# A linear-attention and gated-FFN kernel on one core: batch 0's first k blocks loaded and worked in smaller pieces, loads in another order, the last output in two column parts, and a new work order

## The chip, the cores and the metric

The kernel runs on one core of a Trainium2 chip. The metric is device time in microseconds, the median of several executions. Beside the times there is one profiled execution, with its trace.

## What is computed

For each of 8 batches and 8 heads there are 576 tokens of 64 numbers in q, k and v. A feature map turns q and k into 256 features, linear attention is done with these, and the result (4608 tokens of 512 numbers) goes through a gated FFN.

```
def phi(x):
    proj = einsum('bhsd,df->bhsf', x, w_phi)          # 64 -> 128
    proj = proj - max(abs(proj), axis=-1)
    return concatenate([exp(proj), exp(-proj)])       # 256 features
q_p, k_p = phi(q), phi(k)
kv  = einsum('bhsf,bhsd->bhfd', k_p, v);  z = sum(k_p, axis=2)
num = einsum('bhsf,bhfd->bhsd', q_p, kv); den = einsum('bhsf,bhf->bhs', q_p, z) + 1e-06
x   = (num / den), heads side by side                 # (4608, 512)
out = (maximum(x @ w_gate, 0) * (x @ w_val)) @ w_out  # d_ff = 1536
```

## The kernel before

Matmuls are in bfloat16. All work is cut into small steps called atoms. Each is registered with a number, and a long string, `ORDER`, names the numbers in the order in which the instructions are emitted. As every engine works through its own queue in order, this string fixes the order on TensorE, VectorE, ScalarE, GpSimd and in the DMA queues (SyncE's and GpSimd's) alike. An apostrophe behind a number picks the other engine for a step that two can do, and `z4` emits four fill matmuls of zeros (line 197).

**k of batches 0 and 1.** The 576 tokens of a pair of heads lie as nine blocks (`CP`) of 128 rows, so a batch has four pairs (`NU`) and 36 blocks (`NB`). `k_batch` cuts them into items of eight blocks, 8, 8, 8, 8 and 4. The atoms of item u of batch b are:

- `kT` transposes on TensorE (line 268); `kTc` copies the result to SBUF as tile tT (line 281), on VectorE, or on ScalarE with the apostrophe.
- `kr` projects with w (line 309), into two PSUM banks; `km` takes the row maxima mk on VectorE (line 316), one for each bank; `ke` takes exp of plus and minus the projection on ScalarE (line 365), into tile kp.
- `kk` takes exp of plus and minus the maxima on ScalarE (line 376), tile ek; `vs` scales v by ek (lines 325 and 407), on GpSimd, or on VectorE with the apostrophe.
- `kv` (line 501) multiplies kp with vs, two pairs at a time, over all their blocks; `kvc` (line 415) copies the result.

The tiles kp and vs come from rings of five buffers each. In batches 2 to 7 the transposes are done by DMA and an item is two heads (line 478 for `kv`).

**q.** A `q_item` covers half of a batch's 512 main tokens per head. `qT`, `qTc` are transposes and copies (batches 0 and 1 only); `qc` (line 539) and `qr` (line 309) project, once for the exponentials `qe` (line 557) and once for the maxima `qm` (line 316); `qk` (line 573) is the correction; `n` (line 587) multiplies with kv; `nt` (line 606) and `nu` (line 618) combine the two halves on VectorE; `xu` (lines 625 and 627) divides; `xT` and `xc` (line 647) turn the result for the FFN on TensorE, or `xd` (line 635) by DMA. The last 64 tokens of every head go through tail items and a ninth FFN group.

**FFN.** For each group g, `fv` and `fg` (matmuls at line 717) multiply by w_val and w_gate; `fv` copies on ScalarE or VectorE (line 732), `fg` multiplies on VectorE (line 739); `fo` (line 765) multiplies by w_out in three thirds, and the last third copies the result (line 775) and stores it. In group 0 the first four chunks are done on half of the tokens each (`FIRST`). The weights come through GpSimd's DMA queue in thirds: `wv0`, `wg0` and so on. The last store (group 8, t = 3) is issued in two halves of 64 rows, on SyncE's and ScalarE's queues (line 750).

**The first loads.** Batch 0's k and v come in fp32 over SyncE's queue, k of a pair ahead of its v. GpSimd's own loads (all with a cast) are held back by a tiny copy:

```
for lo, hi in ((0, 1), (1, 2), (2, NU)):
    load_pairs(0, "kn", k, nc.sync, FP32, lo, hi, buf="vn1")
    load_pairs(0, "vn", v, nc.sync, FP32, lo, hi, buf="vn0")
...
gate = singles.tile([P, 1], FP32)
nc.gpsimd.tensor_copy(gate, inputs["kn", 0][:, CP * D : CP * D + 1])
for par in range(2):
    nc.vector.tensor_copy(w2[half_rows(par)], wf)
```

The element that `gate` reads is the first of pair 1. In the trace the fp32 k tile goes by the name of its buffer, vn, as v does.

Of the kernel before, what the change touches and what calls it, by code (L numbers as in the profile page):

```python
# [8 lines left out]
FP32 = mybir.dt.float32  # L9
# [7 lines left out]

FIRST = ((0, 2, 0, 4), (2, 4, 0, 4), (0, 4, 4, 12))

LAST = ((0, 512),)  # L20
# [3 lines left out]
ORDER = """z4 82 83' z1 84 87 86 92 7 8 0 93' 88 85 89 z1 94 95 97 122 123 102 112 1 96 124 98 103 104 99 113  # L24
108 127 90 125 129 105 114 118 91 107 109 115 106 z5 138 100' 177 101 117 139 141 128 126 116 140
178 143 119 186 188 130 142 111 190 110 132 133' 144 145 146 148 147 151 134 150 149 10 120 180 184
152 179 121 131 182 135 137' 153 181 165 154 166 155 167 136 156 29 185 2 159 157 3 191 183 160 187
54 158 226 161 227' 9 171 172 162 168 169 173 216 217' 170 198 199 174 236 256 257 228 192 200 193
189 195 196 237' 194 197 163 164' 246 247' 311 207 208 175 176 209 210 211 201 272 204 205 312' 232
212 206 213 1082' 1083 1084 273' 1085 1086 231 4 1087 1088 202 203 214 215' 218 314 229 233 316 318  # L30
222 1089 1090' 1091 1092 1093 5 220 221 1094 1095 230 219 1096 1097 1098 238 242 239 6 258 259 248
260 261 263 11 223 241 252 243 1099 1100' 250 234 251 240 1101 1102' 249 225 1103 262 1104 1105 320
322 224 324 253 280 244' 254' 284 274 276 282 1106' 1107 1108 1109 264 278 1110 313 255 275 279 317
245 235 266 277 267' 268 281 285 283 30 315 265 269 270 13 351 355 350 319 325 271 321 323 1111
1112' 353 1113 341 338 339 344 342 343 39 1114 1115 340 329 330 345 352 326 331 332 333 354 346 334
299 1116 327 347 305 286 290 291 1117 287 12 328 363 306 356 1118 300 335 51 302 364 365 307 288
1119 303 304 301 308 348 349 293 40 289 1120 1121 292 360 1122 294 295 296 309 310' 361 362 336
1123 388 398 400 337 14 368 371 31 297 298 1124 369 399 372 390 1125 1126 401 16 41 403 389 370 404
1127 1128 402 373 1129 374' 33 58 62 378 381 379 1130 1131 42 1132 405 15 391 380 383 61 393 395
1133 1134 1135 392 394 59 357 358 359 1136 1137 1138 63 415 419 414 418 416 1139 417 1140' 1141 382  # L40
60 64 1142 1143 408 412 409 411 413 410 450 452 454 1144 384 396 397 385 386 387' 375 376 444 377'
448 449 451 443 446 406 420 432 407' 1145 453 438 445 65 1146 447 433 439 440 435 427 428 436 437
455 434 441 442 1147 32 1148 473 474 470 471 472 424 425 426 1149 429 421 422 423 467 468 1150 1151
469 475 1152 456 476 459 498 477 500 460 488 501 430 462 463 464 431 457 490 1153 1154 461 458 465'
502 492 466 499 489 1155 1156 1157 525 519 521 52 503 504 523 19 527 524 528 1158 1159 529 526 1160
491 508 511 478 554 556 510 558 479 482 493 481 509 17 505 530 1161 506 507 1162' 1163 512 513 480
1164 1165 55 559 563 494 560 518 522 483 562 564 565 1166 1167 561 520 1168' 1169 484' 66 69 67 44
43 553 555 557 1170' 1171 515 514 516 517 485 495 496 486 487' 1172' 497 583 577 1173 68 36 70 534
535 536 1174 22 580 581 578 366 367 584 531 579 582 532 1175 1176 566 567 568 548 549 1177 585 586
21 545 587 542 18 546 533 537 538 539 543 544 550 34 547 1178 1179 1180 1181 1182' 589 626 628 588  # L50
591 1183 551 552 569 592 590 540 541 627 1184' 629 570 631 630 1185 1186 1187 572 595 571 593 594
573 1188 574 575 71 1189 1190 576 20 596 597 636 637 616 617 620 72 606 607 619 640 609 1191 1192
1193 608 639 621 598 599 1194' 1195 1196 600 622 618 610 647 46 651 611 612 681 683 641 643 642 685
653 657 53 649 1197' 655 638 1198' 1199 1200' 1201 644 645 652 656 688 690 613 682 686 614 623 624
684 601 602 625' 615 603 692 654 1202' 1203 646 648 687 1204' 633 632 634 635' 650 691 1205 1206'
1207 1208 665 658 662 676 677 689 673 666 45 674 35 667 663 664 1209 670 671 672 1210 659 678 1211
1212 23 660 675 679 680 47 726 728 729 756 758 56 727 731 1213 1214 1215 1216 661 732' 668 669 705
693 706 707 711 712 708 1217 1218 709 710 713 730 760 1219 714 1220' 1221 746 747 736 739 733 750
715 694 695 696 740 738 748 749 700 701 702 25 1222 1223 1224' 697 698 699 703 737 741 1225 1226
704 716 719 718 720 763 73 792 794 717 796 751 767 1227 743 765 1228 1229 1230 1231 762 766 752 757  # L60
791 721 742' 764 744 795 38 759 761 768 793 1232 1233' 753 1234 1235 723 1236' 745 754 755' 734 798
735 797 26 799 722' 827 829 802 1237 1238 831 800 810 48 803 811 807 808 809 775 812 776 801 1239
# [54 lines left out]
def kernel(  # L117
# [20 lines left out]
    nc = tc.nc  # L138
# [4 lines left out]
    P = 128  # L143
# [681 lines left out]
```

## Time and profile before

| | |
|---|---|
| median of 3 runs | 381.93 us (381.91 to 382.31) |
| profiled execution | 382.19 us, of which the span of the profile 380.3 us |
| TensorE busy | 365.8 us (96%) |
| VectorE busy | 294.0 us (77%) |
| ScalarE busy | 215.2 us (57%) |
| GpSimd busy | 139.2 us (37%) |
| TensorE's granted clock, mean | 0.998 |
| DMA | 45.10 MB, mean 119 GB/s |

All times in the profile are in us from the start of the span, unless marked ns. A row of a timeline has start, length, engine, line, operation, output and inputs, count, and in brackets the idle time of the engine before it with what ended it. The length of a merged row reaches to the end of its last instruction; instructions of one engine overlap a little, so the step from one start to the next is often shorter than one instruction's length.

### The profile page before, as it was taken

The numbers are of one execution on the slowest core, as the hardware profiler recorded it, in microseconds if no ns is written. First come the engines' busy times: TensorE is split into PE (matmuls) and PEld (weight loads), VectorE is DVE, ScalarE is ACT, GpSimd is POOL, SyncE is SP. The second block draws the span as 40 slices with busy tenths as digits, with TensorE's granted clock in tenths as the row PEclk, the third lists the DMA queues.
The fourth block names the chain that finished last, engine by engine and source line by source line (L and its number), as shares of the span: only waits on it lengthen the run. The fifth ranks groups of instructions, "written<-read, shape, count | busy, mean of one in ns | idle before, by whom it ended". The sixth has DMA issues, their size and how long they took to land.

```text
span 380.3 us, 8896 instructions
## 1 busy us (share of the span) xinstructions
PE 365.8 (96%) x3447; PEld 196.7 (52%) x3495; DVE 294.0 (77%) x640; ACT 215.2 (57%) x505; POOL 139.2 (37%) x183
## 2 busy tenths in 40 slices
PE   6879999999999999999999999999999999999995
PEld 2558455545544645554555555565554544444442
DVE  3988989888887899989969987989858925836530
ACT  4998994678589647665875459771864112000111
POOL 3976462458265325722580244853400110000000
PEclk9999999999999999999999999999999999999999
DMA  7999997995359989983759743570310220021003
GB/s 245 189 181 236 197 143 149 227 212 154 28 117 196 161 242 162 175 104 73 125 113 148 202 125 96 83 82 16 97 56 16 29 97 28 2 69 55 2 27 84
DMA packets 87625, 45.10 MB, mean 119 GB/s; under 512 B 55776, under 2 KB 81440, under 8 KB 87584
## 3 DMA queue, kind: packets, MB, share of 16 engines
q1 hardware_dynamic: 59984, 30.42, 35.7%
q0 software_dynamic: 27200, 13.57, 27.8%
q10 hardware_dynamic: 400, 0.56, 0.5%
q8 instruction: 27, 0.44, 0.5%
q14 instruction: 14, 0.11, 0.1%
HBM read 37.78 MB, written 9.44 MB: 124 GB/s over the span
## 4 chain that ended last, share of the span: by engine, by line
PE 88%; ACT 4%; DVE 3%; issue 2%; DMA 1%; SPq 0%; DVEq 0%
PE pa L717 45%; PE pa L765 24%; PE pa L587 5%; PE pa L309 5%; PE pa L478 4%; PE pa L539 2%; PE pa L268 2%; DVE h L739 2%; ACT kp L365 2%; DMA vn<-in_k_dram 1%; ACT qp L557 1%; PE pa L501 1%; ACT tT L281 1%; DVE mk L316 1%; DVE val_sb L732 0%
## 5 line engine op out<-in xcount | busy, mean ns | idle before, releaser
L739 DVE SCALAR_TENSOR_TENSOR h<-pa,val_sb 128x512 bf16<-128x512 f32 (+1 forms) x112 | 74.4, 668 | 33.2 <-PE pa L717 24.1
L717 PE MATMUL pa<-xT,wg_sb 128*128 128x512 bf16 (+1 forms) x387 | 98.1, 370 | 0.7
L717 PE MATMUL pa<-xT,wv_sb 128*128 128x512 bf16 (+1 forms) x385 | 97.9, 370 | 0.6
L765 PE MATMUL pa<-wo_sb,h 128*128 128x512 bf16 x414 | 96.7, 379 | 1.2 <-issue 0.3
L732 ACT CAST val_sb<-pa 128x512 bf16<-128x512 f32 (+1 forms) x65 | 37.8, 581 | 81.7 <-PE pa L717 81.4
L557 ACT ACTIVATE qp<-pa 128x512 bf16<-128x512 f32 x144 | 76.1, 625 | 10.3 <-PE pa L539 8.3
L365 ACT ACTIVATE kp<-pa 128x512 bf16<-128x512 f32 (+1 forms) x148 | 76.7, 617 | 9.2 <-PE pa L309 7.7
L627 POOL TENSOR_TENSOR xu<-u,r 128x512 bf16<-128x512 f32 x30 | 31.6, 1058 | 119.1 <-DVE r L625 78.6
L325 POOL TENSOR_TENSOR vs<-vn,ek 128x512 bf16<-128x512 f32 (+1 forms) x58 | 60.0, 1041 | 34.0 <-ACT ek L376 28.1
L717 PEld LDWEIGHTS <-wg_sb 128*128 128x128 bf16 x448 | 41.8, 98 | 45.1 <-issue 2.1
L717 PEld LDWEIGHTS <-wv_sb 128*128 128x128 bf16 x448 | 41.8, 98 | 44.7 <-issue 1.5
L765 PEld LDWEIGHTS <-h 128*128 128x128 bf16 x432 | 40.1, 98 | 45.0 <-issue 0.3
L316 DVE TENSOR_REDUCE mk<-pa 128x4 f32<-128x512 f32 (+1 forms) x74 | 46.9, 667 | 6.0 <-PE pa L309 5.2
L316 DVE TENSOR_REDUCE mq<-pa 128x4 f32<-128x512 f32 x72 | 46.2, 681 | 5.7 <-PE pa L309 5.6
L618 DVE TENSOR_TENSOR u<-pa,t 128x195 f32<-128x195 f32 (+3 forms) x120 | 37.9, 332 | 3.3
L606 DVE TENSOR_TENSOR t<-pa,cq 128x195 f32<-128x195 f32 (+3 forms) x120 | 37.7, 326 | 3.3 <-ACT cq L573 1.5
L775 ACT COPY out_sb<-pa 128x512 f32<-128x512 f32 x21 | 12.7, 603 | 44.5 <-PE pa L765 42.5
L587 PEld LDWEIGHTS <-qp 128*128 128x128 bf16 x640 | 27.5, 98 | 12.2 <-issue 0.6
L732 DVE CAST val_sb<-pa 128x512 bf16<-128x512 f32 (+1 forms) x47 | 31.6, 673 | 2.5 <-PE pa L717 1.6
L587 PE MATMUL pa<-kv,qp 128*128 128x65 bf16 x640 | 30.0, 193 | 0.4 <-ACT qp L557 0.3
L775 DVE COPY out_sb<-pa 128x512 f32<-128x512 f32 x15 | 10.3, 689 | 21.6 <-PE pa L765 18.1
L478 PEld LDWEIGHTS <-kp 128*128 128x128 bf16 x480 | 16.4, 98 | 3.8 <-issue 1.2
(67 smaller groups left out, 273.4 us busy)
## 6 DMA issues: line engine op xcount, KB each, us to landing
out_dram<-out_sb SPq DMA_DIRECT2D x32, 256.0 KB, 2.6
vn<-in_v_dram SPq DMA_DIRECT2D x6, 1024.0 KB, 6.0
qn<-in_q_dram POOLq DMA_DIRECT2D x8, 512.0 KB, 7.5
kn<-in_k_dram POOLq DMA_DIRECT2D x6, 512.0 KB, 7.7
wv_sb<-in_moe_w_val_dram POOLq DMA_DIRECT2D x3, 512.0 KB, 6.9
wg_sb<-in_moe_w_gate_dram POOLq DMA_DIRECT2D x3, 512.0 KB, 9.0
wo_sb<-in_moe_w_out_dram POOLq DMA_DIRECT2D x1, 1536.0 KB, 15.7
vn<-in_v_dram SPq DMA_DIRECT2D x1, 1152.0 KB, 9.2
```

What stands on the lines that cost most here:

```text
L316: nc.vector.tensor_reduce(m, some.rearrange("p (c f) -> p c f", f=F), axis=AX.X, op=ALU.max, apply_absolute_value=True,)
L325: eng.tensor_tensor(dst[:, :, s, 0:D], src, ek[:, :, s : s + 1].to_broadcast(list(src.shape)), op=ALU.mult,)
L365: nc.scalar.activation(st["kp"][:, s, 0 : n // 2, par, :], st["banks"][par][:, 0 : n // 2 * F].rearrange("p (a f) -> p a f", f=F), AF.Exp, ...
L478: nc.tensor.matmul(kv_ps[:, hh, s, :], lhsT=lhsT, rhs=rhs, start=(n == 0), stop=(n == 19))
L557: nc.scalar.activation(x["qp"][:, s, slot].rearrange("p a b -> p (a b)"), st["cols", i][par], AF.Exp, scale=sign,)
L587: nc.tensor.matmul(pn[:, E * (2 * i + s) : E * (2 * i + s + 1)], lhsT=x["qp"][:, s, slot, blk, :], rhs=kv_of(b, lo + i)[:, s, :],)
L606: nc.vector.tensor_tensor(x["t", j][rows, 0:n], ab[:, :, 1], c[:, :, None].to_broadcast([np_, n, E]), op=ALU.mult,)
L618: nc.vector.tensor_tensor(x["u"][rows, lo : lo + n], ab[:, :, 0], x["t", j][rows, 0:n], op=ALU.add)
L717: nc.tensor.matmul(ps, lhsT=w[:, dc, P * fi : P * fi + P], rhs=xTs[g][:, dc, lo:hi], start=(dc == 0), stop=(dc == NDC - 1),)
L732: copy_by(copy_of(alt, "ACT", "DVE"))(st["val", n], ps)
L739: nc.vector.scalar_tensor_tensor(st["h2"][:, fi, lo:hi], ps, 0.0, st["val", n], op0=ALU.max, op1=ALU.mult)
L765: nc.tensor.matmul(po, lhsT=st["h2"][:, fi, P * t : P * t + P], rhs=wo_sb[:, fi, c0:c1], start=(fi == 0), stop=(fi == NFC - 1),)
```

## The change

- `K_CUTS` sets where the items of batches 0 and 1 are cut. Batch 0 now has six items, of 4, 4, 8, 8, 8 and 4 blocks; batch 1 keeps 8, 8, 8, 8, 4. `kv_pairs` looks up an item and a block in a list, `place`.
- Batch 0's k and v are loaded in seven DMAs instead of six: k pair 0 blocks 0 to 3, k pair 0 blocks 4 to 8, k pair 1, v pair 0, k pairs 2 and 3, v pair 1, v pairs 2 and 3.
- `gate` stands as it was, and reads from k pair 1, which is now ahead of v.
- The second half of w2 is copied by ScalarE instead of VectorE.
- The last output is done in two column parts, 352 and 160, each with its own twelve matmuls, copy and two stores (`LAST`).
- `ORDER` is new throughout. There are 9 fill matmuls instead of 11.

```
+K_CUTS = [[4, 8, 16, 24, 32], [8, 16, 24, 32]]
-LAST = ((0, 512),)
+LAST = ((0, 352), (352, 512))
...
-    def load_pairs(b, name, src, eng, dtype, lo=0, hi=NU, buf=None):
+    def load_pairs(b, name, src, eng, dtype, buf=None, pairs=slice(0, NU), toks=slice(0, CP)):
...
-            out=t.rearrange("p (u n) -> p u n", u=NU)[:, lo:hi],
+            out=t.rearrange("p (u c d) -> p u c d", u=NU, c=CP)[:, pairs, toks],
...
-        items = [
-            k_item(
+        cuts = [0] + K_CUTS[b] + [NB]
+        place = []
+        for u, (lo, hi) in enumerate(zip(cuts, cuts[1:])):
+            st = k_item(
                 b,
                 u,
-                min(8, NB - 8 * u),
-                lambda u=u: blocks(u),
+                hi - lo,
+                lambda lo=lo, hi=hi: blocks(lo, hi),
                 None,
-                lambda u=u: v_blocks(8 * u, min(8 * u + 8, NB)),
+                lambda lo=lo, hi=hi: v_blocks(lo, hi),
             )
-            for u in range(-(-NB // 8))
-        ]
+            place += [(st, c) for c in range(hi - lo)]
...
-                it, c = items[blk // 8], blk % 8
+                it, c = place[blk]
...
-    for lo, hi in ((0, 1), (1, 2), (2, NU)):
-        load_pairs(0, "kn", k, nc.sync, FP32, lo, hi, buf="vn1")
-        load_pairs(0, "vn", v, nc.sync, FP32, lo, hi, buf="vn0")
+    for name, *part in (
+        ("k", slice(0, 1), slice(0, 4)),
+        ("k", slice(0, 1), slice(4, CP)),
+        ("k", slice(1, 2)),
+        ("v", slice(0, 1)),
+        ("k", slice(2, NU)),
+        ("v", slice(1, 2)),
+        ("v", slice(2, NU)),
+    ):
+        src, buf = (k, "vn1") if name == "k" else (v, "vn0")
+        load_pairs(0, f"{name}n", src, nc.sync, FP32, buf, *part)
...
-    for par in range(2):
-        nc.vector.tensor_copy(w2[half_rows(par)], wf)
+    for par, copy in enumerate((nc.vector.tensor_copy, nc.scalar.copy)):
+        copy(w2[half_rows(par)], wf)
```

The start of both orders, with the numbers replaced by names (`ke.0.2.1` is batch 0, item 2, second bank; `ld` is a load). On ScalarE, up to the last `qe` of batch 0 and the copies behind it:

```
before: kTc.0.0' ke.0.0.0 kTc.0.1' ke.0.0.1 kk.0.0 ke.0.1.0 ke.0.1.1 kk.0.1 ke.0.2.1 kk.0.4 ke.0.3.1
  kk.0.2 ke.0.2.0 ke.0.4.1 ke.0.4.0 ke.0.3.0 kk.0.3 qe.0.0.0.0 qe.0.0.0.1 qe.0.0.1.0 kvc.0.0.1 qe.0.0.1.1
  qk.0.0 qe.0.1.0.0 kvc.0.1.0 qk.0.1 qe.0.1.0.1 qe.0.1.1.0 kTc.1.1' kTc.1.0' qe.0.1.1.1 kTc.1.2' xc.0.0'
after:  kTc.0.0' kTc.0.1' ke.0.0.0 ke.0.0.1 kk.0.1 ke.0.1.1 ke.0.1.0 kk.0.0 ke.0.2.1 ke.0.2.0 kk.0.2
  kTc.0.3' kTc.0.4' ke.0.3.1 ke.0.4.0 kk.0.3 ke.0.4.1 ke.0.3.0 kk.0.4 qe.0.0.1.1 qe.0.0.1.0 ke.0.5.0 kk.0.5
  qe.0.0.0.0 ke.0.5.1 qe.0.0.0.1 qe.0.1.0.0 qk.0.0 kvc.0.1.0 qe.0.1.0.1 kTc.1.4' qe.0.1.1.1 qk.0.1
  qe.0.1.1.0 kTc.1.0' kTc.1.3' qTc.1.1' xc.0.0'
```

On GpSimd with its loads, up to batch 0's first `xu`:

```
before: ld.q0 ld.k1 ld.wv0 ld.wg0 vs.0.0.0 vs.0.0.1 vs.0.1.1 vs.0.4.0 vs.0.2.1 vs.0.2.0 ld.q1 vs.0.3.0
  vs.0.3.1 vs.0.4.1 ld.qm0 ld.wv1 ld.wg1 xu.0.0.0
after:  ld.q0 ld.k1 vs.0.1.0 ld.wv0 ld.qm0 vs.0.2.0 vs.0.0.1 vs.0.3.0 vs.0.3.1 ld.q1 vs.0.4.0 vs.0.4.1
  vs.0.5.0 vs.0.5.1 ld.wg0 ld.wv1 ld.wg1 xu.0.0.0
```

106 lines of the change are left out of this document (42 added, 64 removed), and 29 rows, old and new, of the table ORDER.

## The prediction, made before the changed kernel was run

> **What bounds the kernel now.** I read the busy time by stretches first, then the chain that ended last, then the timelines of the first 31 us and of the last 15 us. Columns below: the stretch, its length, busy us of TensorE, weight load, VectorE, ScalarE and GpSimd, granted clock, DMA share, GB/s.
>
> ```profile
> 0.00:8.30 8.30, 5.16 (x22) 2.47 (x22) 3.78 (x7) 2.95 (x4) 2.13 (x9) 1.00 0.72 241
> 8.30:16.00 7.70, 7.14 (x60) 4.61 (x59) 6.30 (x12) 7.32 (x22) 7.05 (x11) 1.00 1.14 195
> 16.00:30.70 14.70, 11.56 (x301) 8.83 (x299) 13.03 (x38) 14.55 (x36) 10.48 (x15) 1.00 1.31 187
> 30.70:60.00 29.30, 29.05 (x379) 18.30 (x381) 26.98 (x55) 25.62 (x65) 16.65 (x22) 1.00 1.20 194
> 60.00:375.80 315.80, 312.94 (x2692) 162.47 (x2735) 243.89 (x531) 164.16 (x383) 102.92 (x128) 1.00 0.55 104
> 375.80:380.30 4.50, 0.00 (x0) 0.00 (x0) 0.00 (x0) 0.57 (x1) 0.00 (x0) 0.87 0.29 87
> ...
> 1.65 5.46 DMA vn<-in_k_dram
> 30.73 3.21 PE pa L717 x28
> 370.41 5.36 PE pa L765 x24
> 375.79 0.58 ACT out_sb L775
> ```
>
> TensorE is the bound from 30.7 us on: it idles 0.25 us of 29.3 and 2.86 us of 315.8. The rest of its idle time lies at the ends: 3.14 us before 8.3, 0.56 us to 16, 3.14 us to 30.7, and 4.5 us behind its last matmul. In the stretch from 16 to 30.7 ScalarE is busy 14.55 of 14.70 us: there the exponentials set the pace and TensorE follows. The chain begins with a load of k, pair 1, and is TensorE from 30.73, where the first FFN matmul starts. So the change can gain in three places: the time at which that matmul starts (the work put before it is the same set of matmuls in both orders, less two fill matmuls), the 3.1 us of idle time behind it, and the tail.
>
> **The loads.** The first rows of the start, and the issues of the loads with their us from issue to landing:
>
> ```profile
> 3.92 1.09 PE L268 MATMUL pa<-ident,vn 128*128 128x128 f32 x4 [1.04 <-DMA vn<-in_k_dram]
> 4.03 0.47 DVE L794 CAST w<-wf 64x128 bf16<-64x128 f32 x2 [0.72 <-DMA wf<-in_w_phi_dram]
> 5.04 0.59 ACT L281 CAST tT<-pa 128x512 bf16<-128x512 f32 x1 [2.43 <-PE pa L268]
> 5.68 0.61 PE L309 MATMUL pa<-w,tT 64*128 64x128 bf16 x8 [0.25 <-ACT tT L281]
> 6.33 1.08 ACT L365 ACTIVATE kp<-pa 128x512 bf16<-128x512 f32 x2 [0.70 <-PE pa L309]
> 7.16 0.19 POOL L792 COPY gate<-vn 128x1 f32<-128x1 f32 x1 [5.50 <-DMA vn<-in_k_dram]
> ...
> vn<-in_k_dram SPq DMA_DIRECT2D x1, 288.0 KB, 3.0
> vn<-in_v_dram SPq DMA_DIRECT2D x1, 288.0 KB, 3.4
> vn<-in_k_dram SPq DMA_DIRECT2D x1, 288.0 KB, 5.5
> ```
>
> The third load, k pair 1, was issued at 1.65 with 576 KB ahead of it and took 5.5 us. Now it is still third, but with 288 KB ahead, as the second load had, which took 3.4 us: it lands at 5.05 (4.65 by the first row, 7.15 by the third). The gate at 7.16 and GpSimd's loads behind it then move up by 2.1 us. v pair 0 takes over the later place; its reader needs the k maxima first, at about 6.6 below.
>
> The first exponential moves too. Two transposes instead of four in front of the copy save 0.54 (half of 1.09), a half-size copy 0.22 (half of 0.59, less some fixed time), half the projections 0.26 (0.61 less 0.35), and a 128 KB load instead of 288 KB at most the 0.2 us until w arrives at 4.03. 6.33 less 1.2 is 5.1. The two halves of w on two engines lie in that wait for w and are worth nothing further; without that cover the extra ScalarE copy costs it 0.24 us, half of the row of two. SP issues seven loads now; the added issue (0.50 on the ACT queue in the tail below) stands ahead of v and of k pairs 2 and 3, whose readers come behind 6.6 us; uncovered it would cost that 0.50.
>
> **ScalarE up to the last q exponential of batch 0.** Prices are the steps from one start to the next:
>
> ```profile
> 8.30 0.58 ACT L281 CAST tT<-pa 128x512 bf16<-128x512 f32 x1 [0.89 <-PE pa L268]
> 8.78 1.09 ACT L365 ACTIVATE kp<-pa 128x512 bf16<-128x512 f32 x2
> 15.01 3.17 ACT L365 ACTIVATE kp<-pa 128x512 bf16<-128x512 f32 x8
> 17.97 0.40 ACT L376 ACTIVATE ek<-mk 128x8 f32<-128x8 f32 x2
> 18.17 3.12 ACT L557 ACTIVATE qp<-pa 128x512 bf16<-128x512 f32 x6
> 21.03 0.53 ACT L415 CAST kv<-pa 128x260 bf16<-128x260 f32 x1
> 21.28 1.26 ACT L557 ACTIVATE qp<-pa 128x512 bf16<-128x512 f32 x2
> ...
> 27.97 0.68 ACT L281 COPY tT<-pa 128x512 bf16<-128x512 bf16 x1
> 30.03 0.41 DVE L647 COPY xT<-pa 128x512 bf16<-128x512 bf16 x1
> ```
>
> Six q exponentials take 2.86 (18.17 to 21.03), so 0.48 each and 0.96 a pair. Of the eight of k from 15.01 to 17.97 four are of four blocks: (2.96 - 4 x 0.48)/4 = 0.26 each, 0.52 a pair. A pair of ek is 0.20, a kv copy 0.25, a copy of transposes 0.48. Before, ScalarE took 19.67 us from its second copy at 8.30 to the end of its last q exponential, where the copy at 27.97 follows. In the new order that stretch, begun at the first exponential, has four more half pairs and one full pair less (+2.08 - 0.96), one more ek pair (+0.20), one kv copy less (-0.25), and of copies two fp32 and a half more against three fewer (0.96 + 0.27 - 3 x 0.48 = -0.21, the half one an estimate): +0.86, so 20.53 us. From 5.1 that ends at 25.6; with 0.5 us for its new small waits (the first ek now wants VectorE's maxima of the second item, and the sixth k item wants the first one's buffer of a ring of five, which the first kv product frees) 26.1 against 27.97: 1.8 us earlier. Behind it two copies of 512 columns and one of 1024 (1.9, as four of 0.48) stand before the xT copy (0.48) that now releases the FFN; that still puts the release at 28.5, against the VectorE copy that started at 30.03, ended at 30.44 and released the matmul at 30.73.
>
> **GpSimd is the nearer bound.** The last kv product of batch 0 wants GpSimd's last v product, which ended at 21.59:
>
> ```profile
> 19.68 1.05 POOL L325 TENSOR_TENSOR vs<-vn,ek 128x512 bf16<-128x512 f32 x1
> 20.67 0.25 POOL L407 CAST vs<-ek 128x16 bf16<-128x16 f32 x1
> 20.82 0.61 POOL L325 TENSOR_TENSOR vs<-vn,ek 128x256 bf16<-128x256 f32 x1
> 21.38 0.21 POOL L407 CAST vs<-ek 128x8 bf16<-128x8 f32 x1
> L211 POOL DMA_DIRECT2D qn<-in_q_dram x2: 952/1012/1071, 7.3 to 17.7; - x2
> ```
>
> Now its fourth item waits for ScalarE's ek of that item, which by the prices above comes 7.7 us behind 5.1 (four half pairs, four full ones, four ek pairs, two copies: 2.08 + 3.84 + 0.80 + 0.96), with 0.7 us of waits at 13.5. From there GpSimd does two items of 2 x 0.99 + 0.15, one of 2 x 0.56 + 0.21 and, queued between them, the issue of the next q, 0.95: 6.55, with 0.35 for slower ones beside VectorE 20.4. That is 1.2 us earlier than 21.59. Behind it both orders do the same kv product, normalisations and transposes. I take the nearer bound: **start -1.2 us** (ends -2.1, the gate's shift, and 0, if VectorE gives it all back: it has 13.03 of 14.70 us and gets two more products, less some copies).
>
> **The annealed rest.** The idle time behind 30.7 is 3.1 us, so at most that is gained; as much could be lost. By my count of the two orders, TensorE changes between 64-row and 128-row work 66 times instead of 68, and the spacing from each load to its first use is alike. I take **0** (-1 to +2). What I found tighter is batch 1's last transpose by TensorE: by an estimate of the matmuls that stand between it and batch 1's FFN in each order, it has 1.1 us instead of 1.95, and a copy as the one of 0.41 at 30.03 must fit in between.
>
> **The tail.** Rows of the last 15 us and, last, a 256-column copy of the start:
>
> ```profile
> L775 DVE COPY out_sb<-pa x1: 692/692/692, 373.3 to 373.3; 128x512 f32<-128x512 f32 x1
> 376.40 0.50 ACTq L750 DMA_DIRECT2D out_dram<-out_sb  x1
> out_dram<-out_sb ACTq DMA_DIRECT2D x1, 128.0 KB, 2.6
> L732 DVE CAST val_sb<-pa 128x256 bf16<-128x256 f32 x1 | 0.4, 378 | 0.0
> ```
>
> VectorE's 692 and 378 ns give 1.23 ns a column: 0.50 us for 352 columns, 0.26 for 160. Twelve matmuls of 160 columns at 160/512 of 5.36/24 take 0.84 us, which hide the first copy and nearly its issues (0.50). The last copy ends 0.32 us sooner than the 0.58 of the chain's last row. A store of 128 KB lands 2.6 us from its issue; one of 160 columns instead of 512 saves between 0 and 0.5, or loses 0.2 behind the first part's; I take 0.2. **Tail -0.5** (-0.1 to -0.8). The Trainium skill (DMA: Bandwidth & Descriptors, the fixed and variable cost under Terms) gives about 2.0 us fixed plus bytes over 436 GB/s per DMA, a rule that speaks against cutting loads and stores; by it an estimate of the smaller store's gain is 0.2, and the 2.6 of this trace agrees with a mostly fixed cost.
>
> **Sum.** -1.2 + 0 - 0.5 = -1.7. The profiled execution took 382.19 (span 380.3 and 1.89 around it), so 380.5; the median of the runs, 381.93, lies 0.26 below it: **380.2**. About 0.2% (0.76 us) can be told from no change.
>
> **Rivals.** *The whole shift* (0.16): the gate's 2.1 us arrive in full, with the tail's 0.5: 379.3. For it speaks ScalarE's 1.8, against it GpSimd's 1.2. *Tail only* (0.16): VectorE or the ring of five takes the start back: 381.4; for it, VectorE's 13.03 of 14.70. *The slower side: the gate weights come late* (0.09). GpSimd issues the first third of w_gate only behind its last v product of batch 0, at 20.4, where it did so ahead of its first:
>
> ```profile
> wg_sb<-in_moe_w_gate_dram POOLq DMA_DIRECT2D x1, 512.0 KB, 13.0
> wv_sb<-in_moe_w_val_dram POOLq DMA_DIRECT2D x1, 512.0 KB, 6.8
> L197 PE MATMUL pa<-zeros x11: 379/608/635, 1.0 to 14.4; 128*128 128x512 bf16 x11
> ```
>
> With 6.8, as the later load, it lands at 27.2, before its first reader at about 29.9; over 9.5 it holds all of TensorE's queue; with 13.0, which it took behind three other loads, the stall is 3.5: 383.7. *The rest is worse* (0.14): stalls like those of 30.7 to 375.8 once more, some 2.7 us: 382.9. *A colder start* (0.05): the early fill matmuls took 608 ns against 379 though the granted clock reads 1.00; with two fewer, TensorE could stay slow into the q stage and lose the start's 1.2 and 0.5 more: 381.9. The Trainium skill (TensorE: Matmul & The Clock Gate, Part 1) says the clock is halved until about 3.4 us of sustained work; these two durations fit it.
>
> **Numbers.** The forecast has 0.40 (379.7 to 380.9). Faster by over 0.2%: forecast and whole shift, 0.56; slower: the late weights and most of the worse rest, 0.20; within: tail only, the colder start and the remainder of the worse rest, 0.24. Range 379.0 to 382.9: from the whole shift with the tail's better end to the worse rest.
>
> **What would show it.** Right: the gate near 5 us, the first exponential near 5.1, GpSimd's last v product near 20.4, the first FFN matmul near 29.5, the last copy 0.26 us long. Wrong: that matmul at 30.5 or later, idle TensorE in front of a w_gate matmul, or over 4 us of idle between it and the last matmul.

## The result: slower by 1.4%, and the profile after

| | median us (range) | ratio to before, 95% interval |
|---|---|---|
| before, beside it | 382.08 (381.91 to 382.31) | |
| changed kernel | 387.31 (386.66 to 388.84) | 1.0142 [1.0111, 1.0173] |

The forecast of 380.2 and its range up to 382.9 are both missed, and on the other side. The profiled execution took 386.66 us, 4.47 more than the profiled one of before. Busy times by stretches of the changed kernel, with the columns of the prediction's first fence; the last row ends with its last matmul:

```profile
0.00:8.30 8.30, 5.92 (x35) 2.58 (x36) 5.68 (x12) 5.94 (x18) 4.00 (x12) 1.00 0.79 247
8.30:16.00 7.70, 5.46 (x54) 3.34 (x54) 7.29 (x12) 6.30 (x17) 5.58 (x8) 0.78 1.26 220
16.00:30.70 14.70, 11.26 (x303) 8.74 (x298) 13.87 (x43) 14.70 (x37) 10.47 (x16) 1.00 1.26 218
30.70:60.00 29.30, 27.71 (x368) 17.45 (x372) 24.96 (x49) 23.67 (x62) 15.91 (x21) 1.00 1.15 177
60.00:380.40 320.40, 314.81 (x2710) 164.12 (x2753) 246.27 (x525) 172.69 (x393) 104.88 (x124) 1.00 0.56 102
```

TensorE idles 1.59 us from 30.7 to 60 (0.25 before) and 5.59 from 60 to its end (2.86 before). Some 3 us in either profile are not idle time: behind the first FFN matmul both lack the records of 48 matmuls (3080 are there, and 3068 before, where profiles with all records have 3128 and 3116). So only the differences count. The loss, then, is in the part that the prediction put at 0. In this execution the start did what was forecast; from the timelines:

```profile
4.63 0.94 ACT L368 ACTIVATE kp<-pa 128x256 bf16<-128x256 f32 x3
5.28 0.19 POOL L804 COPY gate<-vn 128x1 f32<-128x1 f32 x1 [3.62 <-DMA vn<-in_k_dram]
20.77 0.21 POOL L410 CAST vs<-ek 128x8 bf16<-128x8 f32 x1
20.90 0.82 POOL L243 DMA_DIRECT2D wg_sb<-in_moe_w_gate_dram  x1
29.71 0.60 PE L721 MATMUL pa<-xT,wv_sb 128*128 128x256 bf16 x4 [0.18 <-ACT tT L284]
30.68 0.61 PE L721 MATMUL pa<-xT,wg_sb 128*128 128x256 bf16 x4 [0.36 <-DMA wg_sb<-in_moe_w_gate_dram]
```

The first FFN matmul starts at 29.71 instead of 30.73; the next group, though, waits for w_gate. From that matmul to the end of the last one it is 350.8 us instead of 345.0: 1.0 us gained, 5.7 lost. What TensorE waited for from 29 us on, by the view of waits (sum, times, longest); before has one entry there, issue, 0.3 (that one and the entry of L769 below stand where records are missing; profiles with all records have neither):

```profile
PE pa L721 <- DMA xT<-xu: 1.4, 1, 1.4
PE pa L591 <- issue: 1.4, 1, 1.4
PE pa L721 <- DVE h L743: 0.8, 2, 0.6
PE pa L769 <- issue: 0.5, 3, 0.2
PE pa L721 <- DVE mq L319: 0.4, 1, 0.4
PE pa L721 <- DMA wg_sb<-in_moe_w_gate_dram: 0.4, 1, 0.4
```

And where they stand, from the timelines of TensorE and VectorE and, third, the chain of waits:

```profile
57.02 0.19 PE L591 MATMUL pa<-kv,qp 128*128 128x65 bf16 x1
58.58 0.64 PE L591 MATMUL pa<-kv,qp 128*128 128x65 bf16 x15 [1.37 <-issue]
110.30 7.47 DMA xT<-xu
118.01 1.02 PE L721 MATMUL pa<-xT,wv_sb 128*128 128x512 bf16 x4 [1.41 <-DMA xT<-xu]
157.38 2.12 DVE L328 TENSOR_TENSOR vs<-vn,ek 128x512 bf16<-128x512 f32 x1
160.16 1.02 PE L721 MATMUL pa<-xT,wg_sb 128*128 128x512 bf16 x4 [0.37 <-DVE mq L319]
163.49 1.02 PE L721 MATMUL pa<-xT,wg_sb 128*128 128x512 bf16 x4 [0.56 <-DVE h L743]
381.32 0.32 DVE L779 COPY out_sb<-pa 128x160 f32<-128x160 f32 x1 [1.06 <-DMA out_dram<-out_sb]
```

Besides w_gate there are four places: a pause of TensorE at 57.2 for which the trace shows no releaser; a turned tile of batch 2 that took 7.47 us from issue to landing; two waits behind a v product of 2.12 us on VectorE; and the last copy, which waits 1.06 us for a store.

### The profile page after: what moved, and what is told of

Its sections match the earlier page's. It is cut to its first block, busy times and chain, and to the rows that moved or that the text cites. A ratio compares the mean times of both kernels' runs of the same rounds, so it can differ in the third digit from the quotient of the medians.

```text
span 384.9 us, 8951 instructions
## 1 busy us (share of the span) xinstructions
PE 365.2 (95%) x3457; PEld 196.2 (51%) x3505; DVE 298.4 (78%) x639; ACT 223.3 (58%) x524; POOL 140.8 (37%) x178
## 4 chain that ended last, share of the span: by engine, by line
PE 83%; DVE 6%; DMA 5%; ACT 3%; issue 2%; POOL 1%; SPq 0%; DVEq 0%
PE pa L721 47%; PE pa L769 21%; PE pa L591 5%; PE pa L482 4%; PE pa L312 3%; DMA wg_sb<-in_moe_w_gate_dram 3%; DMA xT<-xu 2%; PE pa L543 2%; ACT kp L368 2%; DVE vs L328 2%; DVE mk L319 1%; DVE t L610 1%; DVE u L622 1%; DMA out_dram<-out_sb 1%; DVE mq L319 1%
## 5 line engine op out<-in xcount | busy, mean ns | idle before, releaser
L769 PE MATMUL pa<-wo_sb,h 128*128 128x512 bf16 (+2 forms) x429 | 97.4, 373 | 1.2 <-issue 0.5
L736 ACT CAST val_sb<-pa 128x512 bf16<-128x512 f32 (+1 forms) x75 | 43.0, 573 | 82.1 <-PE pa L721 81.1
L769 PEld LDWEIGHTS <-h 128*128 128x128 bf16 x444 | 41.2, 98 | 46.0 <-issue 1.1
L736 DVE CAST val_sb<-pa 128x512 bf16<-128x512 f32 (+1 forms) x37 | 25.0, 677 | 6.1 <-PE pa L721 5.5
L779 DVE COPY out_sb<-pa 128x512 f32<-128x512 f32 (+2 forms) x16 | 10.5, 653 | 24.1 <-PE pa L769 22.8
```

Source lines behind the costliest of these rows:

```text
L736: copy_by(copy_of(alt, "ACT", "DVE"))(st["val", n], ps)
L769: nc.tensor.matmul(po, lhsT=st["h2"][:, fi, P * t : P * t + P], rhs=wo_sb[:, fi, c0:c1], start=(fi == 0), stop=(fi == NFC - 1),)
```

## The experiments

**Theory 1**: the loss lies in the new order behind the first FFN matmul, as separate stalls, and the start is as good as forecast. **Rival 2**: the new start costs the time later. **Rival 3**: the tail's split costs. All runs, with their ratios, and from their profiles the start of the first FFN matmul, the us from it to the end of the last matmul, and the us from there to the end of the span (an end is the last row's start plus its length). Kernels that ran together share the runs of before; those medians lay between 381.8 and 382.4.

| kernel | us | ratio, 95% interval | first FFN | to last matmul | tail |
|---|---|---|---|---|---|
| before | 382.08 | | 30.73 | 345.0 | 4.6 |
| changed | 387.31 | 1.0142 [1.0111, 1.0173] | 29.71 | 350.8 | 4.4 |
| new_start_old_rest | 382.70 | 1.0025 [1.0001, 1.0048] | 29.70 | 345.4 | 4.6 |
| old_start_new_rest | 386.44 | 1.0117 [1.0083, 1.0150] | 30.37 | 350.6 | 4.7 |
| tail_split | 381.92 | 1.0004 [0.9986, 1.0023] | 30.23 | 345.1 | 4.5 |
| tail_split_own | 381.00 | 0.9966 [0.9949, 0.9984] | 29.93 | 346.1 | 3.7 |
| after_turns | 388.15 | 1.0154 [1.0118, 1.0189] | 30.19 | 351.2 | 4.9 |
| after_ffn_between | 387.24 | 1.0130 [1.0106, 1.0154] | 30.69 | 350.5 | 4.5 |
| after_wg0_early | 386.43 | 1.0116 [1.0094, 1.0137] | 30.65 | 349.8 | 4.4 |
| after_vs_pool | 385.29 | 1.0080 [1.0054, 1.0106] | 29.70 | 348.7 | 4.4 |
| after_six_fills | 390.08 (one time) | | 30.62 | 353.2 | 4.5 |
| after_repaired | 384.49 | 1.0064 [1.0045, 1.0083] | 31.14 | 347.3 | 4.2 |
| best | 382.76 | 1.0014 [0.9998, 1.0030] | 30.66 | 346.7 | 3.9 |
| start_swap | 382.06 | 0.9993 [0.9977, 1.0008] | 29.46 | 345.9 | 4.6 |
| best_swap | 381.12 | 0.9967 [0.9952, 0.9983] | 30.23 | 345.0 | 3.9 |
| after_repaired_swap | 384.57 | 1.0058 [1.0035, 1.0081] | 29.69 | 348.8 | 4.2 |
| old_start_repaired_rest | 384.58 | 1.0059 [1.0040, 1.0077] | 30.11 | 348.9 | 3.9 |
| after_no_dve_vs | 384.92 | 1.0072 [1.0051, 1.0094] | 30.07 | 348.4 | 4.6 |
| repaired_no_dve_vs | 383.39 | 1.0042 [1.0015, 1.0070] | 29.69 | 347.0 | 3.7 |
| best_no_dve_vs | 382.93 | 1.0007 [0.9994, 1.0021] | 29.71 | 347.6 | 3.7 |

### Which part: the start, the rest, the tail

```
new_start_old_rest:  changed kernel; ORDER = new up to fv.0.0, then before's;  LAST = ((0, 512),)
old_start_new_rest:  before;         ORDER = before's up to fv.0.0, then the new one
tail_split:          before;         LAST = ((0, 352), (352, 512)), with fo.8.3.1.* at the end
```

> The changed loads, six items for batch 0 and the new order up to the first FFN matmul, then the old order for everything behind it; the last output whole. Theory 1 (the loss lies in the new order behind the start): the first FFN matmul comes near 29.7 as in the changed kernel, w_gate may still hold TensorE for about 0.5 us, and the rest costs what it did before: 381.0 us, between 380.5 and 381.7. Theory 2 (the smaller items and the late w_gate load cost the 5 us): 384 us or more.

> The old loads, items and order up to the first FFN matmul, then the new order for everything behind it; the last output whole. Theory 1: 386 to 388 us, with TensorE idle some 4 us longer between the first FFN matmul and the last matmul than before. Theory 2: within 1 us of the kernel before, 381.5 to 383.

> The kernel before with the last output in two column parts and nothing else. Ring theory (two output buffers: the copy of the last 160 columns must wait until the store of the third output block has landed): no gain, 381.7 to 382.3, and the last copy is released by a DMA. The prediction's step (copy 0.3 us shorter, store 0.2 us quicker): 381.4 to 381.6, the last copy released by TensorE.

The new order of the rest alone, with the old start, gives 1.0117; the new start alone 1.0025, where 381.0 us was expected of it; the split alone nothing. As to the part, theory 1 stands, and rivals 2 and 3 fall. The same pause and the same VectorE waits are there with the old start, by old_start_new_rest's view of waits:

```profile
PE pa L587 <- issue: 1.4, 1, 1.4
...
PE pa L717 <- DVE h L739: 0.8, 2, 0.6
```

### The tail

```
tail_split_own (= tail_split and this):
-  out_sb = sb_g.tile([P, DM], FP32, name="out_sb", bufs=2)[:, 0 : c1 - c0]
+  if part == 0: out_sb = sb_g.tile([P, DM], FP32, name="out_sb", bufs=2)[:, 0 : c1 - c0]
+  else:         out_sb = sb_g.tile([P, c1 - c0], FP32, name="out_tail", bufs=1)
```

> The kernel before with the last output in two column parts, the second part copied into a small buffer of its own. Ring theory: the last copy is released by TensorE at once, the tail behind the last matmul falls from 4.5 to about 4.0 us, and the time is 381.2 to 381.5 if the kernel before is at 381.8. If the landing of the last store sets the end whatever its size: 381.6 to 382.0, tail 4.4 or more.

The last copy of tail_split, and of tail_split_own, from VectorE's timelines:

```profile
376.23 0.32 DVE L775 COPY out_sb<-pa 128x160 f32<-128x160 f32 x1 [1.16 <-DMA out_dram<-out_sb]
```

```profile
376.02 0.33 DVE L778 COPY out_tail<-pa 128x160 f32<-128x160 f32 x1 [0.25 <-PE pa L765]
```

The output tiles have two buffers; for a third there is no room in SBUF (tail_split_ring3: a pool of 10 KB per partition, where 8.94 are left), so the second part gets a small one of its own. Split, the last output makes one copy more in the last microseconds, and this must wait for the store of the tile two before it. With a buffer of its own it waits 0.25 us, for TensorE; the tail is 3.7 us, and the kernel is faster than before by about 1 us: 0.9966 [0.9949, 0.9984]. The split's gain is real; the ring of two hid it.

### The stalls of the rest, one at a time

```
after_turns:        ld.v3 moved right behind turn.k.3;  turn.qm.1 moved right behind xd.2.2
after_ffn_between:  fv.0.15 fg.0.15 moved right behind kv.1.1 (between batch 1's two kv products)
after_wg0_early:    ld.wg0 moved right behind ld.wv0
after_vs_pool:      vs.4.0.0' -> vs.4.0.0   (GpSimd instead of VectorE)
```

> The changed kernel with two steps moved in the DMA queues: the load of batch 3's v goes out before batch 2's turned outputs, and the turn of the q tails behind the last of them. Queue theory (batch 2's last turned output lands 7.5 us after its issue, because it shares the DMA engines with that load and that turn): the wait of 1.4 us in front of batch 2's FFN falls under 0.3 and the time to about 386. If the transposes are slow by themselves: wait and time stay, 387.3.

> The changed kernel with one FFN step (eight matmuls of 512 columns) moved up between the two kv products of batch 1, so that TensorE uses up fewer instructions in a microsecond there. Fetch theory (the idle 1.4 us at 57 us, with no wait, is TensorE's next block of instructions arriving late): the gap shrinks to under 0.5 us, time about 386. If a hidden wait for data holds TensorE there: the gap stays at 1.2 to 1.6 us, 387.3.

> The changed kernel with GpSimd's load of the first third of w_gate issued right behind that of w_val, instead of behind batch 0's last v product. If the late load costs what the trace shows: no wait in front of the second FFN matmul group (0.5 us before), 386.6 to 387. If the load's place in the queue only moves the wait to the next q load behind it: no gain, 387.3.

> The changed kernel with one v product, of item (4,0), done by GpSimd instead of VectorE. If the product of 2.12 us on VectorE beside GpSimd's own is what holds VectorE's queue up to the h at 162.7: the two waits of TensorE for h and for mq near 157 to 163 (1.2 us together) are gone, TensorE busy 9.9 of 10 us between 160 and 170, time 1.0 to 1.2 us below the changed kernel (ratio near 1.011). If GpSimd itself is the bound there, the waits stay or turn up as waits for GpSimd's vs, ratio 1.013 to 1.015.

In all but after_ffn_between the wait aimed at is gone; only after_vs_pool moved the time beyond the intervals. The stretch from 110 to 120 in the changed kernel, and in after_turns:

```profile
110.00:120.00 10.00, 8.44 (x67) 3.89 (x66) 8.38 (x15) 8.22 (x23) 5.24 (x7) 1.00 1.01 171
```

```profile
110.00:120.00 10.00, 9.84 (x83) 4.75 (x79) 8.86 (x16) 8.82 (x21) 5.40 (x6) 1.00 0.94 164
...
59.70:63.10 3.40, 3.40 (x15) 1.27 (x12) 1.45 (x4) 0.00 (x0) 0.00 (x0) 0.50 0.03 5
...
PE pa L590 <- issue: 2.1, 1, 2.1
```

The 1.4 us are back there, but the time stayed. In that execution the first FFN matmul came 0.5 later, the pause near 58 was 2.1 us instead of 1.37, and behind it the granted clock was 0.50 from 59.7 to 63.1, where eight matmuls of 512 columns took 3.35 us instead of 1.73. Nor is the queue shown to be what made the tile late. Without the edit it took 2.6 to 7.5 us from issue to landing in the seven profiles of the new rest; with it 2.5 here and in after_repaired, but 6.7 in after_repaired_swap and 7.1 in old_start_repaired_rest.

after_wg0_early has no w_gate wait, but its issue stands in GpSimd's queue ahead of its last v product, which ends at 21.91 instead of 20.98, and the first FFN matmul is at 30.65: it seems one wait traded for another, though the same start without this edit gave 29.70 to 30.69.

after_vs_pool was worth 2.4 us by the times (1.0142 less 1.0080; about 0.8 to 3.9 by the two intervals), where 1.0 to 1.2 was expected; the stretch from 160 to 170 in the changed kernel and in after_vs_pool:

```profile
160.00:170.00 10.00, 9.22 (x98) 5.08 (x99) 8.53 (x18) 6.00 (x13) 7.06 (x10) 1.00 0.78 119
```

```profile
160.00:170.00 10.00, 10.00 (x118) 5.54 (x116) 7.83 (x13) 7.22 (x15) 6.94 (x10) 1.00 0.81 135
```

The two waits there, 0.37 and 0.56 us, are gone. In that execution the turned tile was on time too, 5.1 us behind its issue, though nothing ahead of it had been edited, and that is another 1.4. So one v product on VectorE cost 0.9 us by the waits behind it; that the rest of the 2.4 is its doing is not shown. Of its 2.12 us on VectorE 0.7 are what such a product takes where GpSimd is free.

### The pause near 58 us

```
after_six_fills:  the second z1 -> z7   (six more fill matmuls, twelve TensorE instructions with their weight loads)
```

> The changed kernel with six more fill matmuls (multiplications of zeros into a scratch bank) in the wait for the first k: TensorE's instruction numbers all move up by twelve, the work and its data stay. Theory fetch (the pause near 58 belongs to a place in TensorE's instruction stream): it stays at the same instruction number, so it stands twelve instructions earlier in the program, in the last q products or the kv product's end ahead of the normalisation where it stood. Theory data (the normalisation waits for something that the trace does not show): the pause stays in front of the normalisation's second matmul group, whatever its number. Time as the changed kernel, 386 to 388.

```profile
56.33 0.37 PE L542 MATMUL pa<-tT,w 64*128 64x512 bf16 x1
59.31 0.39 PE L542 MATMUL pa<-tT,w 64*128 64x512 bf16 x1 [2.61 <-issue]
```

The pause left the normalisation (line 591, between its first and second matmul) and stands twelve instructions earlier in the program, inside a pair of q products. Counted from TensorE's first record, weight loads, matmuls and the sequencer's own alike, the first instruction that is held up is number 1474 there and in after_vs_pool; in the changed kernel it is 1471, behind three missing matmul records. In after_ffn_between, too, it stayed (0.98 us, at 1471 with the same three missing) while the program there was another; the copy that its row names is the last event that the profile had. So it belongs to a place in TensorE's instruction stream and not to that work or its data.

The other profiles tell what it waits for. The 20 profiles have 22 such pauses, of 0.17 to 2.61 us, and all stand at number 450, 706 or 1474, which lie 256 and 3 x 256 apart. Before has one as well, 0.69 us at 22.94. Among the queues is one for instructions, with packets of 0.44 MB / 27 = 16 KB; in the changed kernel the fifth was moved from 55.99 to 57.12. The queue in the whole execution, and from 55.98 to 57.13:

```profile
q8 instruction: 27, 0.44, 0.5%
...
q8 instruction: 1, 0.02, 6.1%
```

At all 22 pauses TensorE goes on 1.2 to 1.6 us behind the end of a packet: the first packet at number 450, the second at 706, the fifth at 1474. So it waits there for its next block of instructions. The Trainium skill (Runtime: NRT & Kernel Launch, Instruction fetch mechanics) says that the sequencer fetches blocks of 16 KiB, 256 instructions, over a DMA queue of its own, and that a crossing is mostly hidden. The packet size and the step of 256 agree; 1.37 and 2.61 us in these traces are not hidden. The 256 instructions ahead of number 1474 hold batch 1's two kv products, 144 short matmuls of some 2.5 us, in both orders. In after_vs_pool, with the new order, they are worked off in 3.8 us, the pause not counted; in tail_split, with the old one and without a pause there, in 4.3, and number 1474 starts 1.6 us behind its packet. So the old order is near the edge too, and that the new one outruns its instructions there fits; no run was made to show it.

### All repairs, and the start again

```
after_repaired:  after_wg0_early + after_turns + after_ffn_between + after_vs_pool + tail_split_own's buffer
best:            new_start_old_rest + ld.wg0 right behind ld.wv0 + tail_split_own's tail
```

> The changed kernel with all the repairs at once: w_gate's first third issued behind w_val's first third, the load of batch 3's v earlier so that batch 2's fourth turned output is issued with its neighbours, the FFN group moved between the two kv products of batch 1, the v product of item (4,0) on GpSimd instead of VectorE, and the fourth output's second part copied into a buffer of its own. Theory 1 (the loss is a sum of separate stalls of TensorE, each with its own cause: 0.5 us w_gate, 1.4 turned output, 1.2 the h wait near 163, 1.1 the store in front of the last copy, 1.4 the pause near 58): the first four go, 4.0 us off the changed kernel, 382 to 383, about the time of before. Theory 2 (the stalls only show where a too tight order catches up, and one that is removed turns up later as another): 386 and above, with new waits of more than 1 us in other places between 60 and 300.

> The new start with w_gate's first third issued behind w_val's first third, the old order behind the first FFN matmul, and the last output split with a buffer of its own for its second part. If both gains are real and add up: the start's 1.0 us and the tail's 1.0 to 1.3 us off the kernel before, ratio 0.9945 to 0.996 (379.9 to 380.4). If the start's gain does not reach the end even without the w_gate wait, because a pause of TensorE further on takes it back: as the kernel with the tail alone, 0.9966. If the early issue only delays w_val's first third as much as it speeds w_gate's: first FFN matmul 0.4 us later, ratio 0.996 to 0.998.

Together the repairs take 2.8 us off the changed kernel, less than the 4 that theory 1 summed, and best has not both gains: its first FFN matmul is at 30.66, and behind it stand a pause of 0.64 at 58.3 (number 1474 again) and a wait of 0.67 for h at 82. Two questions were left: where the start's gain goes, and what remains of the rest.

```
start_swap:               new_start_old_rest with ld.qm0 and ld.wg0 in each other's place, turn.qm.0 right ahead of ld.v1
best_swap:                start_swap with tail_split_own's tail
after_repaired_swap:      after_repaired with that exchange instead of the early ld.wg0
old_start_repaired_rest:  old_start_new_rest + the three repairs of the rest + tail_split_own's tail
```

> The new start with the places of two of GpSimd's loads exchanged, the old order behind it, the last output whole: w_gate's first third is issued where the two loads of q's tails stood (about 8.7 us), the tails' loads where it stood (behind the last v product), and the turning of the tails stands right ahead of batch 1's v load. Theory queue (what GpSimd issues ahead of its last v product sets the first FFN matmul; the late w_gate then eats it up): the tails' two issues (1.39 us) give way to one of 0.75, last v product of GpSimd at 20.3, first FFN matmul at 29.1 to 29.4, no wait for w_gate, ratio 0.995 to 0.998. Theory start elsewhere (the start's gain is lost in a stretch behind the first FFN matmul, whatever w_gate does): ratio 1.000 to 1.003, first FFN matmul as early, but 346 us and more from it to the last matmul.

> As start_swap, with the last output split and a buffer of its own for its second part. If both gains hold and add up: 1.0 to 1.5 us of the start and 1.0 of the tail, ratio 0.993 to 0.9955 (379.4 to 380.4). If the start's gain does not hold: 0.9966 as the tail alone.

> The changed kernel with all repairs, w_gate's first third by the exchange of places instead of being added early. Theory queue: first FFN matmul 29.1 to 29.7 instead of 31.14, the rest as in after_repaired (347.3 us from it to the last matmul): 382.3 to 383.2, ratio 1.000 to 1.002. If the pause tied to TensorE's instruction number comes back with the other start: 1 us more, 1.003.

> The start of before, behind it the new order with its three repairs (batch 3's v load earlier, the FFN group between batch 1's kv products, the v product of item (4,0) on GpSimd), the last output split with its own buffer. If the repaired rest is as good as the old one: as the kernel before with the tail alone, 0.9966. If a remainder belongs to the rest itself: 1 to 2 us above that, 0.999 to 1.002, and 346.5 to 348 us from the first FFN matmul to the last matmul. If the repairs only work with the new start: as old_start_new_rest less the tail, 1.008 to 1.009.

**The start.** start_swap has the earliest first FFN matmul of all, no w_gate wait, and the time of before; the tail alone (0.9966) and the tail with this start (0.9967) are alike. Three things took the start's 1.0 us. First, the profiled execution of before was a late one: four other profiles of the same start have the gate at 5.66, 5.92, 6.76 and 6.39 instead of 7.16 and the first FFN matmul at 30.23, 29.93, 30.37 and 30.11 instead of 30.73. tail_split's gate:

```profile
5.66 0.19 POOL L792 COPY gate<-vn 128x1 f32<-128x1 f32 x1 [3.99 <-DMA vn<-in_k_dram]
```

Second, the new start spreads as well: the six profiles with the changed kernel's own start have the first FFN matmul at 29.70 to 30.69, against 29.93 to 30.73 in the five of the old one, 0.3 us earlier by the medians. Third, at 80 us start_swap's TensorE waits for VectorE's h:

```profile
80.14 1.02 PE L720 MATMUL pa<-xT,wv_sb 128*128 128x512 bf16 x4 [0.73 <-DVE h L742]
```

That wait is in four of the seven profiles of the old order's rest (0.29, 0.67, 0.73, 0.86), and what decides it is one v product on VectorE at 77 us. Here are VectorE's and GpSimd's rows around it in tail_split, without the wait, and in tail_split_own, with 0.86 of it:

```profile
75.56 1.06 POOL L325 TENSOR_TENSOR vs<-vn,ek 128x512 bf16<-128x512 f32 x1
77.14 0.69 DVE L325 TENSOR_TENSOR vs<-vn,ek 128x512 bf16<-128x512 f32 x1 [0.27 <-ACT ek L376]
77.97 1.07 POOL L325 TENSOR_TENSOR vs<-vn,ek 128x512 bf16<-128x512 f32 x1
```

```profile
76.83 2.05 DVE L325 TENSOR_TENSOR vs<-vn,ek 128x512 bf16<-128x512 f32 x1 [0.28 <-ACT ek L376]
76.90 1.06 POOL L325 TENSOR_TENSOR vs<-vn,ek 128x512 bf16<-128x512 f32 x1
```

Where GpSimd is at no product when VectorE's starts, it takes 0.69 us; where GpSimd is at a product of its own (or begins one 0.07 us later, as in tail_split_own), it took 1.46 to 2.05 in the four profiles with the wait. Three of the four with it started the FFN below 30 us; without it none did, so an earlier start seems to bring the two together, but best, at 30.66, has it as well.

**What remains of the rest.** With all repairs it is 348.8 us with the new start and 348.9 with the old, 3.8 more than best_swap's 345.0. after_repaired_swap's largest waits from 31 to 378 us are for VectorE; best_swap has none there but for missing records:

```profile
PE pa L720 <- DVE mq L318: 0.9, 2, 0.5
...
PE pa L504 <- DVE h L742: 0.4, 1, 0.4
PE pa L311 <- DVE u L621: 0.3, 1, 0.3
```

VectorE's v products of 512 columns from 31 us on, before and changed (count, busy, mean ns of one):

```profile
L325 DVE TENSOR_TENSOR vs<-vn,ek 128x512 bf16<-128x512 f32 x9 | 6.5, 730 | 0.3 <-ACT ek L376 0.3
```

```profile
L328 DVE TENSOR_TENSOR vs<-vn,ek 128x512 bf16<-128x512 f32 x9 | 11.1, 1237 | 2.2 <-ACT ek L379 2.2
```

Nine of them in both, 4.6 us more of VectorE's time in the new order, since there six of the nine start while GpSimd is at a v product of its own, and before only two. So theory 1 gave way to **theory collision**: the new order pairs VectorE's v products with GpSimd's, and what queues behind them comes late.

```
after_no_dve_vs:     changed kernel; vs.1.0.1' 3.0.1' 3.1.1' 3.3.1' 4.0.0' 5.0.0' 5.2.0' 7.1.0' 7.2.1' without the apostrophe
repaired_no_dve_vs:  after_repaired_swap, the same
best_no_dve_vs:      best_swap, its nine v products of batches 1 to 7 on VectorE likewise
```

> The changed kernel with all nine v products of batches 1 to 7 that VectorE did on GpSimd, nothing else. Theory collision: more than after_vs_pool (1.008), the pause near 58 and the w_gate and turned-tile waits stay: 347 to 348 us, ratio 1.003 to 1.006. Theory order: as after_vs_pool, 1.007 to 1.009.

> after_repaired_swap with all v products of batches 1 to 7 on GpSimd (eight more moved). Theory collision (VectorE's product waits where GpSimd is in an operation; five such products are 3.4 us too long together, and what queues behind them on VectorE makes TensorE wait): the waits for mq, h and u go, 345.5 to 346.5 us from the first FFN matmul to the last matmul instead of 348.8, time 381.5 to 382.7, ratio 0.998 to 1.001. Theory order (these waits come from VectorE's own sequence of maxima, t, u and h): 348 us and more, ratio 1.004 to 1.006. If GpSimd becomes too late: new waits of TensorE for vs, ratio above 1.006.

> best_swap with all v products of batches 1 to 7 on GpSimd (nine moved). In the old order's rest they do not collide, but for the one near 77 us in some executions (0.69 us in four, 1.46 to 2.05 in four others, with a wait of 0.3 to 0.9 us for h behind it). Theory collision: that wait cannot come any more, the rest as it was: ratio 0.995 to 0.997. Theory relief (VectorE with 8 us less work lets TensorE go): 0.993 to 0.995. If GpSimd becomes too late: above 0.998.

With nine v products on GpSimd and nothing else the changed kernel goes from 1.0142 to 1.0072, half of its loss (about 0.0032 to 0.0108 by the two intervals); 1.0080 came already with the one of after_vs_pool. In the repaired order the waits for VectorE shrink to 0.3 and less:

```profile
PE pa L768 <- DVE mq L318: 0.3, 1, 0.3
PE pa L311 <- DVE u L621: 0.2, 1, 0.2
PE pa L720 <- DVE h L742: 0.2, 1, 0.2
```

Its stretch is 347.0 instead of 348.8, its time 1.0042 instead of 1.0058, with intervals that overlap: less than theory collision expected, and its effect on the time beyond the first product is not told apart. How much of the gain is the end of the collisions and how much the mere relief of VectorE, these runs do not tell apart: of the 11.1 us that the nine products took there, some 6 are their length where GpSimd is free. Relief alone is no gain everywhere: the same move makes the old order slower (0.9967 to 1.0007), where TensorE then waits for GpSimd:

```profile
PE pa L481 <- POOL vs L327: 1.0, 1, 1.0
PE pa L481 <- POOL vs L409: 0.9, 1, 0.9
```

What remains of the repaired new order is 2.0 us in the stretch (347.0 to 345.0). Two profiles with all their matmul records split it; the stretch from the first FFN matmul to the last matmul in repaired_no_dve_vs, and in tail_split, whose order there is that of before:

```profile
29.69:376.68 346.99, 345.97 (x3128) 181.83 (x3127) 260.74 (x563) 197.53 (x457) 127.70 (x159) 1.00 0.63 111
```

```profile
30.23:375.28 345.05, 344.95 (x3128) 181.78 (x3127) 271.39 (x586) 189.89 (x445) 119.42 (x150) 1.00 0.62 111
```

Half is idle time, 1.0 us instead of 0.1. The other half is TensorE's own: the same 3128 matmuls keep it busy 1.0 us longer, so they overlap one another less. **Still open** is which neighbourhoods of the order cost that overlap.

## Why the prediction was wrong, point by point

- **The annealed rest, 0 (-1 to +2): the step that failed.** It measured +5.7 us by the profiles, and by itself 1.0117 of the time (4.5 us). It took its bound from the idle time that was there to be gained, 3.1 us, and said that as much could be lost. That idle time was not there: it is the 48 missing records, and tail_split, with the same order and all of them, idles 0.10 of 345.05 us. So there was nothing to gain, and nothing bounds a loss at what can be gained. By the changed kernel's rows the loss is the pause for instructions (1.4), the turned tile (1.4; why it landed late stays open), the two waits behind the v product (0.9), w_gate (0.4), smaller waits and, by after_vs_pool's profile against tail_split's, 0.8 us more of TensorE's own time for the same matmuls. The prediction's two counts (changes between 64-row and 128-row work, spacing of loads and first uses) look at none of these: not at which engine works beside which, not at the place of short matmuls in the instruction stream. The one tight place that it named, batch 1's last transpose by TensorE, is not among the waits.
- **The rival "rest is worse"** had the sign and the place, at 0.14, with a price of 2.7 us, half of what came.
- **The start, -1.2:** right against the profiled execution (-1.02; GpSimd's last v product ended at 20.98 against 20.4, the gate 5.28 against 5.05, the first exponential 4.63 against 5.1). But the load of 5.5 us was that one execution's: other profiles of the same start show GpSimd idle for 3.99 to 5.10 in its place, and 0.4 to 0.8 of the 1.0 us were never there; so the agreement is in part luck. By the medians of all such profiles the new start is 0.3 us ahead. A part of the shift has another cause than the prediction's: the pause at number 450, in batch 0's kv product, took 0.60 to 0.80 us in the five profiles of the old start and at most 0.35 with the new ones. Nor did it ask who is late next once TensorE comes early: VectorE, at 80 us.
- **The late gate weights (0.09)** came as a mechanism: issued at 20.90, behind the last v product, w_gate held TensorE up, by 0.36 us and not by 3.5.
- **The tail, -0.5:** the copy took 0.32 us (forecast 0.26), but the step left out that the one copy more wants a buffer of a ring of two. As written the split is worth nothing; with its own buffer it is worth 1 us (0.6 to 1.9 by the interval), twice the forecast. The cost rule that the prediction takes from the Trainium skill (DMA: Bandwidth & Descriptors) stands there under Anatomy of one DMA, for GpSimd's path, and not under Terms; these stores go out on SyncE's and ScalarE's queues.
- **Colder start (0.05):** the granted clock did fall, to a mean of 0.78 from 8.3 to 16 us, and the first FFN matmul was early all the same. Of the fills that took 608 ns the prediction says that the clock reads 1.00; before's trace has no record of the clock ahead of 13.9 us. Where the records read 0.50, in other profiles, such a matmul took 616 to 634 ns.
- **Range and chances:** the sign came from the two terms that could be worked out; the third, an order new over 345 us, got the width of a small one. Its own sign of being wrong, more than 4 us of idle time between the first FFN matmul and the last, came.

## What to carry to other kernels

An order that is new over the whole program is not a term of 0 because the work is the same: give it the widest range of all, to the losing side above all, and look in it for the steps that two engines do at once on the same kind of data, and for runs of short matmuls. Before you take idle time for room, count the records: a few dozen missing matmuls looked like 3 us here. When a step splits a tile, count once more the buffers of the ring that it uses. And take a gap at the start from several executions before you promise to close it.

## What was not expected of the hardware

**VectorE's product waits for GpSimd's.** The same multiplication takes 0.69 us alone and up to 2.12 (at 157.38) or 2.05 (at 76.83) beside GpSimd's. Behind 31 us the 20 profiles have 149 of them. All 71 that start within a v product of GpSimd took 0.82 to 2.58 us, and most ended 0.54 to 0.56 us behind that product. Of the other 78 all but three took 0.68 to 0.70, beside GpSimd's casts and DMA issues too; in the three, GpSimd's product began within 0.41 us. The Trainium skill (GPSIMD Engine Reference, Specifications) says that GpSimd shares its SBUF interfaces with VectorE, with contention where VectorE has two SBUF inputs; this operation has two, and the trace agrees.

**TensorE pauses at numbers of its instruction stream**, 450, 706 and 1474 in these kernels, for 0.17 to 2.61 us, whatever work stands there, and goes on 1.2 to 1.6 us behind the end of an instruction packet.

**The granted clock falls to half** for 3.4 us within the first 25 us in nine of the 20 profiles, at no cost that shows there. In the changed kernel, whose first FFN matmul is at 29.71:

```profile
12.00:14.00 2.00, 1.89 (x13) 0.99 (x12) 2.00 (x6) 0.89 (x2) 0.27 (x1) 0.50 1.23 208
```

Where TensorE is the bound it does cost: 1.6 us in after_turns, from 59.7 on. There and in after_six_fills it fell behind the two longest pauses near 58, 2.10 and 2.61 us; behind the others there, of up to 1.96, it stayed at 1.00.
